# Pack attention fused with SwiGLU on one core: attention's products ahead of W's, half-products summed in place

## The chip, the cores and the metric

One core of a Trainium2 chip runs the whole program. The metric is device time in microseconds (us): the median of three executions. Beside it stands one profiled execution, in which every instruction of every engine has a start and a duration.

The engines are called PE (matrix products; PEld is its weight load), DVE (vector work), ACT (pointwise functions, casts, copies), POOL (slow vector work) and SP (which issues most transfers). Each runs its own instructions in a fixed order and waits at the first one whose inputs, or whose place for the result, are not ready.

## What is computed

```python
def sm_attn(qq, kk, vv):                       # 8 batches, 8 heads, head size 64
    s = scale * np.matmul(qq, kk.transpose(0, 1, 3, 2))
    s = s - np.max(s, axis=-1, keepdims=True)
    a = np.exp(s)
    a = a / (np.sum(a, axis=-1, keepdims=True) + 1e-09)
    return np.matmul(a, vv)
p_packed = sm_attn(p, k, v)                    # 32 pack rows look at 576 tokens
attn = sm_attn(q, p_packed, p_packed)          # 576 tokens look at 32 pack rows
x = attn of all heads side by side             # 4608 tokens x 512
g = x @ w_gate                                 # 512 x 1536
silu = g * (1.0 / (1.0 + np.exp(-g)))
out = (silu * (x @ w_val)) @ w_out             # 1536 x 512
```

All is float32. The large products are made from two parts of each operand, a rounded one ("high") and what is left of it ("low"), so three products stand for one.

## The kernel before

**Tiling.** The batches go through one after the other. Since the second attention has only 32 pack rows per head, its output is never formed: the packed rows are multiplied with w_gate and w_val first ("W's products", `m_mm`, 8 pairs of matmuls 32x512 at L293, result tile `aux`), split into `mh` (ACT, L669) and `ml` (DVE, L611), and the weights of attention `a2h`, `a2l` then multiply these (L712 in batch 1, L1092 from batch 2 on, result tile `gv`).

**Slots.** The inner dimension 1536 is cut into 12 pieces; piece fc of batch b is a slot. PE's order in a slot is written out by hand:

1. chunk a: 12 matmuls of 256 tokens into two banks (gate, val);
2. in odd slots (and in slot 11, for the next batch) W's products for the next pair of pieces;
3. in some slots products of the next batch's attention: q0 and q1 (scores of the pack rows, L433), pack (L517), mm0 and mm1 (scores of the tokens, L293 into `gv_aux`);
4. the first half of the output products of an earlier pair of pieces (`products(.., 0)`, 12 matmuls 256 wide, L1229, or in batch 1 `out_mm`, L731);
5. chunk b: 12 matmuls of 320 tokens into two banks;
6. the second half of the output products (`products(.., 1)`, 9 matmuls).

Behind a chunk ACT makes silu of the gate bank (`sg`, L719 or L1098) and DVE multiplies it with the val bank (`hf`, L723, or a quarter of the tiles `more` and `extra`, L1105).

**Banks.** Chunks, attention and W's products take their banks in turn from a ring of four, two at a time. In an odd slot that carries attention, chunk a has one pair, the next products the other pair, the products after these chunk a's pair again (so they wait for its silu and its product), and chunk b the other pair again (so it waits for the readers of whoever had it).

**Output products.** From batch 2 on, two pieces and two blocks of tokens form a 2x2 block product made from seven products instead of eight. Its left sides are four sums of quarters of the raw product (`ho`, from `split_raw`) and three (`hs`, from `split_sums`). POOL makes the sums, ACT the high part, DVE the low part. Before, POOL writes three of the sums to a tile `s_raw` of its own (L1188, L1197, L1198) and one in place (L1189). `ho` and `hs` have one buffer each.

**Who sets the order.** PE's order is the order of the code. The order on DVE, ACT and POOL is made by a scheduler from its own estimates, except for instructions under `pin`, which keep the order of the code among themselves. What attention does between the products is a table of words: `FIRST` for batch 2, `LATER` for the batches after it. A word's place "1.ha" means slot 1, after the whole of chunk a and its silu; "1.2" means the middle of slot 1, ahead of W's products. The words `q1r` and `q0r` are the readers of scores (maximum L448, subtraction L449, each twice), `block0` and `block1` those of mm0 and mm1 (L550).

**The tail.** Behind the last slot of batch 7 come seven pairs j = 0 to 6 whose two halves of output products are still to do, with five steps of a block of 64 left-over tokens of each batch pair between (`p4_step`, 6 matmuls 512 wide, L731), then `results` (DVE, L1259), and `end_out` (L733 to L749), which brings out the last 128 rows through two tiles x and y.

Of the kernel before, what the change touches and what calls it, by code (L numbers as in the profile page):

```python
# [25 lines left out]
P = 128  # L26
# [10 lines left out]
SCALE = 1.0 / 8.0  # L37
NW = 8 * P
SPLIT = 0
PAD = 0  # L40
QC = DM // 2

FRONT = 320
# [24 lines left out]
    0.2 q0  # L68
    0.4 q0r
    0.b q0s  # L70
    1.ha q1 q0e q1r
    1.6 q0z
    2.a q1e
    2.4 q1z
# [2 lines left out]
    4.2 factors  # L77
    4.5 turn0
    4.hb turn1
    5.ha pack  # L80
    5.b load_k
    6.a load_v
    6.8 tiles
    7.ha mm0 block0
    7.hb max0
    7.8 exp0
    8.1 sums0
    9.ha mm1 block1
# [10 lines left out]
"""  # L99

LATER = """
    -1.ha q0 q0r q0s
    -1.b q0e
    1.ha q1 q1r
    2.a q1e
    2.6 q0z
    2.b q1z
# [26 lines left out]
def tile_pack_attention_swiglu(ctx: ExitStack, tc: tile.TileContext, qT, q0, kT, v, vq, pT, wgv, wout, out):  # L134
# [22 lines left out]
    nc.scalar.activation(warm, zero, AF.Exp)  # L157

    w_t = [
        const.tile([P, NHP * 4 * P], F32, tag=f"w{k}", name=f"w{k}")[:, : NHP * 4 * P].rearrange(  # L160
            "p (h f n) -> p h f n", h=NHP, f=2
        )
        for k in range(NFC // 2)
# [646 lines left out]
    with tc.manual_schedule(engines={mybir.EngineType.PE}):  # L810
# [349 lines left out]
        late, s_raw, u_t, t4_parts = (None,) * 4  # L1160
        parts, accs = {}, {}

        def as_parts(x):
            return x.rearrange("p i (x n) -> p i x n", x=2)

        def open_late():
            nonlocal late, s_raw, t4_parts
            early_stack.close()
            late = ctx.enter_context(tc.tile_pool(name="late", bufs=1, reuse_waits="tile"))
            s_raw = late.tile([P, 3, P], F32, name="s_raw")  # L1170
# [6 lines left out]
        def part_tile(t, n):  # L1177
            x = late.tile([P, 2, n, P], F32R, tag=t, bufs=1, name=t)
            return x[:, 0], x[:, 1]

        def low(dst, src, high):
            nc.vector.tensor_tensor(dst, src, high.bitcast(F32), op=ALU.subtract)  # L1182

        def split_raw(at):

            x = raw[at]
            (a21, a11), (a22, _) = ([x[:, f, t] for t in range(2)] for f in range(2))
            nc.gpsimd.tensor_tensor(s_raw[:, 0], a21, a11, op=ALU.subtract)  # L1188
            nc.gpsimd.tensor_tensor(a21, a21, a22, op=ALU.add)  # L1189
            x = x.rearrange("p f t n -> p (f t) n")  # L1190
            hi, lo = parts[at, 0] = part_tile("ho", 4)
            nc.scalar.copy(hi, x)  # L1192
            low(lo, x, hi)

        def sum_raw(at):
            x = raw.pop(at)
            nc.gpsimd.tensor_tensor(s_raw[:, 1], x[:, 0, 0], x[:, 0, 1], op=ALU.subtract)  # L1197
            nc.gpsimd.tensor_tensor(s_raw[:, 2], x[:, 1, 1], s_raw[:, 1], op=ALU.subtract)  # L1198
            places.append(x)

# [9 lines left out]
        def t_quarter(k, i):  # L1210
            return ts[k][:, 0, i], ts[k][:, 1, i]

        def products(at, which, fill):
# [71 lines left out]
        def batch2(b):  # L1285
            nonlocal u_t, t4_parts
            run = plan_of(b)
            for fc in range(NFC):
# [32 lines left out]
                def half(which):  # L1321
# [36 lines left out]

# [40 lines left out]
```

## Time and profile before

| | us |
|---|---|
| median of three executions | 727.21 (725.76, 727.21, 727.58) |
| the profiled execution | 726.56 |
| its span, first to last instruction | 724.8 |
| outside the span (726.56 - 724.8) | 1.76 |
| PE busy in the span | 704.6 (97%) |
| DVE, ACT, POOL busy | 494.1, 403.1, 175.6 |
| mean granted clock of PE | 0.995 of full speed |

Time is read from the start of the span. PE is busy nearly always, so a change shows where PE stands still, where it runs at a lower clock, and at the very end. Where PE waits, the row of its next matmul says in brackets how long it stood and which instruction it waited for ("3.25 <-DVE e L449").

### The profile page before, as it was taken

How to read it: one execution, taken by the hardware profiler on the slowest of the kernel's cores; microseconds unless marked ns; L12 is line 12 of the kernel's file. 1: busy time of each engine (PE TensorE's matmuls, PEld its weight loads, DVE VectorE, ACT ScalarE, POOL GpSimd, SP SyncE). 2: the span in 40 equal slices, each digit the busy share in tenths (PEclk: the TensorE clock that was granted, in tenths of full speed). 3: DMA queues.
4: the chain of work that ended last, by engine and by line, in shares of the span. 5: the costliest groups of instructions: out<-in, count | busy, mean ns of one | idle time of the engine just before them, and what ended most of it. 6: DMA issues, size and time to landing. Idle time of an engine off the chain costs nothing.

```text
span 724.8 us, 16371 instructions
## 1 busy us (share of the span) xinstructions
PE 704.6 (97%) x6503; PEld 619.5 (85%) x6503; DVE 494.1 (68%) x1093; ACT 403.1 (56%) x714; POOL 175.6 (24%) x349
## 2 busy tenths in 40 slices
PE   7999999999979999999999999999999999999995
PEld 5687788888868999989989899898979989989985
DVE  4986876567856687677657776777746777555453
ACT  3788555635646475745736467655645456444331
POOL 0000000331452222322313323332312322233342
PEclk9999999999999999999999999999999999999999
DMA  9999993010250533434233441442405224210001
GB/s 347 359 350 318 335 419 125 7 73 13 105 186 8 200 124 119 158 143 162 99 126 107 168 171 64 165 182 88 182 17 173 93 88 175 89 60 30 1 30 44
DMA packets 25436, 103.27 MB, mean 142 GB/s; under 512 B 6672, under 2 KB 7952, under 8 KB 16656
## 3 DMA queue, kind: packets, MB, share of 16 engines
q1 hardware_dynamic: 25072, 102.00, 38.5%
q8 instruction: 51, 0.84, 0.5%
q10 hardware_dynamic: 288, 0.23, 0.1%
q14 instruction: 25, 0.20, 0.1%
HBM read 86.44 MB, written 15.78 MB: 141 GB/s over the span
## 4 chain that ended last, share of the span: by engine, by line
PE 89%; DVE 5%; ACT 2%; issue 2%; POOL 2%; DMA 0%; ACTq 0%; SPq 0%; DVEq 0%
PE gv L1092 31%; PE acc L1229 24%; PE acc L731 9%; PE aux L293 6%; PE gv L956 5%; PE gv L712 4%; PE aux L731 3%; PE gv_aux L293 1%; PE gv_aux L517 1%; PE warm_ps L817 1%; PE gv_aux L433 1%; DVE hs L1182 1%; DVE ot L1259 1%; ACT ho L1192 1%; PE gv_aux L854 0%
## 5 line engine op out<-in xcount | busy, mean ns | idle before, releaser
L1092 PE MATMUL gv<-a2h,ml 128*128 128x256 f32 (+1 forms) x576 | 124.5, 298 | 3.2 <-DVE e L449 3.2
L1092 PE MATMUL gv<-a2l,mh 128*128 128x256 f32 (+1 forms) x576 | 124.2, 297 | 0.0
L1092 PE MATMUL gv<-a2h,mh 128*128 128x256 f32 (+1 forms) x576 | 123.9, 296 | 0.0
L1092 PEld LDWEIGHTS gv<-a2h,ml 128*128 128x128 f32 x576 | 91.5, 189 | 4.7 <-issue 3.6
L1092 PEld LDWEIGHTS gv<-a2h,mh 128*128 128x128 f32 x576 | 93.4, 190 | 0.0
L1092 PEld LDWEIGHTS gv<-a2l,mh 128*128 128x128 f32 x576 | 93.2, 189 | 0.0
L611 DVE TENSOR_TENSOR ml<-aux,mh 128x512 fp32r<-128x512 f32 (+1 forms) x94 | 60.5, 676 | 32.6 <-ACT mh L669 32.5
L1203 ACT CAST hs<-s_raw 128x384 fp32r<-128x384 f32 x72 | 36.9, 512 | 76.4 <-PE acc L1229 70.4
L1098 ACT ACTIVATE sg<-gv 128x256 f32<-128x256 f32 (+1 forms) x144 | 59.2, 411 | 35.7 <-PE gv L1092 32.6
L669 ACT CAST mh<-aux 128x512 fp32r<-128x512 f32 (+1 forms) x94 | 50.0, 584 | 38.9 <-PE aux L293 38.4
L1229 PE MATMUL acc<-wo_h,ho 128*128 128x256 f32 x288 | 66.6, 294 | 2.2 <-DVE ho L1182 2.1
L1229 PEld LDWEIGHTS acc<-wo_h,ho 128*128 128x128 f32 x288 | 49.2, 188 | 18.3 <-issue 14.8
L1229 PE MATMUL acc<-t_w,hs 128*128 128x256 f32 x432 | 63.4, 282 | 0.0
L1229 PE MATMUL acc<-t_w,ho 128*128 128x256 f32 x432 | 62.8, 281 | 0.0
L1229 PEld LDWEIGHTS acc<-t_w,hs 128*128 128x128 f32 x432 | 58.6, 188 | 0.9 <-DVE ot L1259 0.2
L1188 POOL TENSOR_TENSOR s_raw<-more 128x128 f32<-128x128 f32 x36 | 16.7, 463 | 166.1 <-DVE hs L1182 163.9
L1229 PEld LDWEIGHTS acc<-t_w,ho 128*128 128x128 f32 x432 | 56.4, 188 | 0.2
L1182 DVE TENSOR_TENSOR hs<-s_raw,hs 128x384 fp32r<-128x384 f32 x72 | 39.6, 550 | 21.9 <-ACT hs L1203 20.8
L1188 POOL TENSOR_TENSOR s_raw<-extra 128x128 f32<-128x128 f32 x36 | 16.9, 469 | 142.3 <-DVE hs L1182 142.3
L1105 DVE TENSOR_TENSOR more<-gv,sg 128x256 f32<-128x256 f32 x72 | 30.1, 418 | 22.0 <-PE gv L1092 10.8
L1192 ACT CAST ho<-more 128x512 fp32r<-128x512 f32 x36 | 22.2, 618 | 33.0 <-PE acc L1229 26.1
L1229 PE MATMUL acc<-wo_l,ho 128*128 128x256 f32 x144 | 40.5, 282 | 0.0
(224 smaller groups left out, 1565.9 us busy)
## 6 DMA issues: line engine op xcount, KB each, us to landing
w_s<-wd SPq DMA_DIRECT2D x36, 1024.0 KB, 5.2
st<-in_wgv SPq DMA_DIRECT2D x12, 1024.0 KB, 7.6
k_t<-in_kT SPq DMA_DIRECT2D x16, 576.0 KB, 5.6
out<-ot SPq DMA_DIRECT2D x35, 256.0 KB, 2.2
q_t<-in_qT SPq DMA_DIRECT2D x14, 576.0 KB, 7.0
v_t<-in_vq SPq DMA_DIRECT2D x6, 1280.0 KB, 7.8
st<-in_wout SPq DMA_DIRECT2D x6, 1024.0 KB, 6.8
wd<-w SPq DMA_DIRECT2D x6, 1024.0 KB, 11.8
```

Source lines behind the costliest of these rows:

```text
L293: nc.tensor.matmul(outs[par][32 * hp : 32 * hp + 32], lhs(r, hp), rhs(r, hp), start=True, stop=True)
L611: pin(nc.vector.tensor_tensor(*x[1], op=ALU.subtract))
L669: nc.scalar.copy(m[0][at], src)
L731: nc.tensor.matmul(acc[:, at], h_[:, c : c + P], w_[fc // 2][:, fc % 2, at], start=((fc == 0 or first) and i == 0), stop=(fc == NFC - 1 an ...
L956: nc.tensor.matmul(held[i][s][:, :n], m_[:, g, f, s * P : (s + 1) * P], a_[:, g, off : off + n], start=(j == 0), stop=(j == len(todo) - 1),)
L1092: nc.tensor.matmul(pg[:, :n], m_[:, g, fc % 2, s * P : (s + 1) * P], a_[:, g, off : off + n], start=(i == 0), stop=(i == 5),)
L1098: nc.scalar.activation(sg[:, :n], pgs[0][:, :n], AF.Silu)
L1105: nc.vector.tensor_tensor(x, pgs[1][:, o : o + 256], sg[:, o : o + 256], op=ALU.mult)
L1182: nc.vector.tensor_tensor(dst, src, high.bitcast(F32), op=ALU.subtract)
L1188: nc.gpsimd.tensor_tensor(s_raw[:, 0], a21, a11, op=ALU.subtract)
L1203: nc.scalar.copy(hi, s_raw)
L1229: nc.tensor.matmul(acc[bank][:, QC * col : QC * col + QC], h_[:, x], w_, start=(k == 0 and i == 0 and col == 0), stop=(k == 5 and i == 2 a ...
```

## The change

Seven things are altered at once.

1. **Tables.** The places of q0, q1, pack, mm0 and mm1 go from "X.ha" to "X.2", in both tables. These products then stand ahead of W's products in the slot, and their readers ahead of `ml`.
2. **Sums in place.** `s_raw` is gone. POOL makes one sum in place (L1192), ACT and DVE make `ho` from the quarters, then POOL makes three sums in place (L1201), one after the other and only after DVE's low part has read the quarters; `hs` is made from these. The place in `more` or `extra` is given back only there. The columns of two products change accordingly.
3. **`split_sums`** is called ahead of chunk a rather than behind it.
4. **`pin_first`** keeps the code's order for the sums of the very first pair.
5. **Two buffers in the tail.** Pairs 1, 3 and 5 of the last half take their `ho` and `hs` from the buffers of `a2h` and `a2l`.
6. **The tail's left-over steps** move by one pair: none at j = 0, one at j = 5. `end_out` takes x and y from tiles no transfer reads any more.
7. **Addresses.** `PAD` is 40 instead of 0, and the tile of one weight block is 80 elements longer. Both only move tiles in memory.

```diff
 FIRST
-    1.ha q1 q0e q1r
+    1.2 q1 q0e q1r
-    5.ha pack
+    5.2 pack
...
 LATER
-    -1.ha q0 q0r q0s
+    -1.2 q0 q0r q0s
-    7.ha mm0 block0
+    7.2 mm0 block0
...
-        x, y = (pool.tile([P, DM], F32, tag="ot", bufs=2, name="ot") for _ in range(2))
+        x, y = (pool.tile([P, DM], F32, tag=t, bufs=1, name="ot") for t in ("a1", "s2"))
...
+        def part_tile(at, t, n):
+            if at[:2] == (B - 1, 1) and at[2] % 2:
+                x = pool.tile([P, 2, n, P], F32R, tag={"ho": "a2h", "hs": "a2l"}[t], bufs=2, name=t)
+            else:
+                x = late.tile([P, 2, n, P], F32R, tag=t, bufs=1, name=t)
...
+        def pin_first(at, ins):
+            return pin(ins) if at == (2, 0, 0) else ins
...
         def split_raw(at):
-            nc.gpsimd.tensor_tensor(s_raw[:, 0], a21, a11, op=ALU.subtract)
-            nc.gpsimd.tensor_tensor(a21, a21, a22, op=ALU.add)
+            x = raw[at].rearrange("p f t n -> p (f t) n")
+            pin_first(at, nc.gpsimd.tensor_tensor(x[:, 0], x[:, 0], x[:, 2], op=ALU.add))
...
         def sum_raw(at):
-            nc.gpsimd.tensor_tensor(s_raw[:, 1], x[:, 0, 0], x[:, 0, 1], op=ALU.subtract)
-            nc.gpsimd.tensor_tensor(s_raw[:, 2], x[:, 1, 1], s_raw[:, 1], op=ALU.subtract)
-            places.append(x)
+            for to, a, b in ((1, 0, 1), (3, 3, 1), (2, 1, 2)):
+                pin_first(at, nc.gpsimd.tensor_tensor(x[:, to], x[:, a], x[:, b], op=ALU.subtract))
...
+                if cur:
+                    split_sums(cur)
                 chunk(b, fc, False, fill, lambda: run(fc, "a"))
                 run(fc, "ha")
-                if cur:
-                    split_sums(cur)
...
-            if j < 5:
-                p4_step(j, B - 1)
+            if 0 < j < 6:
+                p4_step(j - 1, B - 1)
```

**ACT, batch 1, slot 1** (`sg` is silu of chunk a's gate bank, `e_1424` the exponentials of batch 2's first scores q0; a table load goes with each change of function). On PE, q1's row moves above W's in this slot.

```order
 L199 COPY ot<-acc 128x512
-L719 ACTIVATE sg<-gv 128x256
-L199 CAST hh<-hf 128x256
 L455 ACT_TABLE_LOAD
 L455 ACTIVATE e_1424<-e_1424 128x2x2x144
-L669 CAST mh<-aux 128x512 x2
 L719 ACT_TABLE_LOAD
+L719 ACTIVATE sg<-gv 128x256
+L199 CAST hh<-hf 128x256
+L669 CAST mh<-aux 128x512 x2
```

The exponentials and the load of silu's table now stand ahead of chunk a's silu.

**DVE, batch 2, slot 1, before**: the readers of q1's scores (L448, L449).

```order
L630 TENSOR_TENSOR b_t<-wo_h,wo_l 128x1024
L1105 TENSOR_TENSOR more<-gv,sg 128x256
L1182 TENSOR_TENSOR t_first<-t_593,t_first 128x256
L460 TENSOR_REDUCE z_2396<-e_2395 128x2x2
L448 TENSOR_REDUCE z_2396<-gv_aux 128x2
L1182 TENSOR_TENSOR hs<-s_raw,hs 128x384
L449 TENSOR_TENSOR e_2395<-gv_aux,z_2396 128x2x144
L448 TENSOR_REDUCE z_2396<-gv_aux 128x2
L1182 TENSOR_TENSOR t_first<-t_795,t_first 128x256
L449 TENSOR_TENSOR e_2395<-gv_aux,z_2396 128x2x144
L611 TENSOR_TENSOR ml<-aux,mh 128x512 x2
```

**DVE, the same place, of the change.**

```order
L630 TENSOR_TENSOR b_t<-wo_h,wo_l 128x1024
L1105 TENSOR_TENSOR more<-gv,sg 128x256
L1184 TENSOR_TENSOR t_first<-t_593,t_first 128x256
L460 TENSOR_REDUCE z_2373<-e_2372 128x2x2
L448 TENSOR_REDUCE z_2373<-gv_aux 128x2
L449 TENSOR_TENSOR e_2372<-gv_aux,z_2373 128x2x144
L448 TENSOR_REDUCE z_2373<-gv_aux 128x2
L449 TENSOR_TENSOR e_2372<-gv_aux,z_2373 128x2x144
L611 TENSOR_TENSOR ml<-aux,mh 128x512 x2
L1184 TENSOR_TENSOR t_first<-t_795,t_first 128x256
```

`hs` of the first pair no longer stands between the readers, and a left-over split has gone behind `ml`.

**ACT, the start of the tail, of the change** (silu of the last chunk b is the first row; `ho` and `hs` of three pairs follow).

```order
L1098 ACTIVATE sg<-gv 128x320
L1194 CAST ho<-extra 128x512
L1207 CAST hs<-more 128x384
L1249 COPY extra<-acc 128x256
L1207 CAST hs<-extra 128x384
L1250 COPY ot<-acc 128x256
L1194 CAST ho<-more 128x512
L1207 CAST hs<-more 128x384
```

The `ho` that PE needs next (from `more`) stands behind the `hs` of a pair that is needed later (from `extra`); before, it came straight after the two copies.

## Rows read from the trace of the kernel before

**Rows 1.** The page: DVE's group of ml (busy, mean ns, idle before it).
```profile
L611 DVE TENSOR_TENSOR ml<-aux,mh 128x512 fp32r<-128x512 f32 (+1 forms) x94 | 60.5, 676 | 32.6 <-ACT mh L669 32.5
```
**Rows 2.** Timeline of PE, batch 2, slot 1: start, duration, operation, count, [idle before].
```profile
209.42 0.40 PE L731 MATMUL acc<-wo_h,t_first 128*128 128x512 f32 x1
213.06 0.87 PE L1092 MATMUL gv<-a2h,ml 128*128 128x320 f32 x2 [3.25 <-DVE e L449]
...
216.30 0.40 PE L1092 MATMUL gv<-a2h,ml 128*128 128x256 f32 x2
```
**Rows 3.** The chain, 400 to 425 us: chunk b and two halves of output products.
```profile
409.14 1.77 PE gv L1092 x12
...
418.80 1.07 PE acc L1229 x9
...
421.31 1.42 PE acc L1229 x12
```
**Rows 4.** Timeline of DVE at the wait of rows 2.
```profile
208.79 0.44 DVE L448 TENSOR_REDUCE z<-gv_aux 128x2 f32<-128x288 f32 x1
211.99 0.56 DVE L1182 TENSOR_TENSOR hs<-s_raw,hs 128x384 fp32r<-128x384 f32 x1 [2.76 <-ACT hs L1203]
212.46 0.45 DVE L449 TENSOR_TENSOR e<-gv_aux,z 128x288 f32<-128x288 f32 x1
```
**Rows 5.** Timeline of PE, batch 1, slot 1.
```profile
120.82 1.09 PE L293 MATMUL aux<-w,ppt 64*32 64x512 f32 x16
121.70 0.75 PE L433 MATMUL gv_aux<-k_t,p_t 64*32 64x144 f32 x32
122.38 0.51 PE L731 MATMUL acc<-wo_h,hl 128*128 128x512 f32 x1
```
**Rows 6.** Timeline of ACT, the same slot.
```profile
120.26 0.38 ACT L719 ACTIVATE sg<-gv 128x256 f32<-128x256 f32 x1
...
121.88 1.28 ACT L455 ACT_TABLE_LOAD   x1
123.17 0.69 ACT L455 ACTIVATE e<-e 128x576 f32<-128x576 f32 x1
```
**Rows 7.** Timeline of PE, batch 1, slot 5.
```profile
147.75 1.96 PE L293 MATMUL aux<-w,ppt 64*32 64x512 f32 x16
...
150.29 1.31 PE L517 MATMUL gv_aux<-v_t,a 128*32 128x64 f32 x76 [0.34 <-DVE a L505]
151.53 0.50 PE L731 MATMUL acc<-wo_h,hl 128*128 128x512 f32 x1
```
**Rows 8.** Timeline of DVE, the same slot: the second transpose.
```profile
149.40 0.83 DVE L505 STREAM_TRANSPOSE a<-e 128x640 f32<-128x640 f32 x1
```
**Rows 9.** Windows: us; PE, PEld, DVE, ACT, POOL busy; granted clock; DMA share, GB/s.
```profile
213.00:216.50 3.50, 3.44 (x14) 3.47 (x15) 2.17 (x5) 0.64 (x2) 3.00 (x4) 0.55 0.45 174
...
713.00:717.00 4.00, 3.02 (x24) 3.02 (x25) 2.45 (x5) 1.24 (x3) 0.38 (x1) 1.00 0.00 0
```
**Rows 10.** Timeline of PE in the tail.
```profile
690.20 0.40 PE L731 MATMUL aux<-wo_h,t_parts 128*128 128x512 f32 x1
...
697.85 0.39 PE L1229 MATMUL acc<-wo_h,ho 128*128 128x256 f32 x1 [0.70 <-DVE ho L1182]
...
713.98 0.39 PE L1229 MATMUL acc<-wo_h,ho 128*128 128x256 f32 x1 [1.36 <-DVE ho L1182]
```
**Rows 11.** Timeline of ACT in the tail.
```profile
691.24 0.62 ACT L1192 CAST ho<-more 128x512 fp32r<-128x512 f32 x1 [0.82 <-POOL more L1189]
```
**Rows 12.** Timeline of DVE in the tail: low part of ho.
```profile
686.84 0.69 DVE L1182 TENSOR_TENSOR ho<-more,ho 128x512 fp32r<-128x512 f32 x1 [1.63 <-ACT ho L1192]
```
**Rows 13.** Timeline of POOL in the tail.
```profile
691.83 0.46 POOL L1198 TENSOR_TENSOR s_raw<-more,s_raw 128x128 f32<-128x128 f32 x1
```
**Rows 14.** Timeline of DVE at the end.
```profile
718.00 0.75 DVE L1259 TENSOR_TENSOR ot<-acc,ot 128x256 f32<-128x256 f32 x2
720.59 0.36 DVE L745 COPY ot<-aux 128x192 f32<-128x192 f32 x1 [1.83 <-DMA out<-ot]
```
**Rows 15.** Timeline of SP's queue at the end.
```profile
721.43 0.33 SPq L749 DMA_DIRECT2D out<-ot  x1
```

More of the change, by code (lines that the diff above doesn't have):

```diff
@@ L39 @@
 SPLIT = 0
-PAD = 0
+PAD = 40
 QC = DM // 2
@@ L87 @@
     8.1 sums0
-    9.ha mm1 block1
+    9.2 mm1 block1
     9.3 turn_0
@@ L101 @@
 LATER = """
-    -1.ha q0 q0r q0s
+    -1.2 q0 q0r q0s
     -1.b q0e
-    1.ha q1 q1r
+    1.2 q1 q1r
     2.a q1e
@@ L112 @@
     4.ha turn1
-    5.ha pack
+    5.2 pack
     6.7 tiles
-    7.ha mm0 block0
+    7.2 mm0 block0
     7.5 max0
@@ L120 @@
     8.hb turn_0
-    9.ha mm1 block1
+    9.2 mm1 block1
     9.5 high0
@@ L159, in tile_pack_attention_swiglu @@
     w_t = [
-        const.tile([P, NHP * 4 * P], F32, tag=f"w{k}", name=f"w{k}")[:, : NHP * 4 * P].rearrange(
+        const.tile([P, NHP * 4 * P + (80 if k == NFC // 2 - 1 else 0)], F32, tag=f"w{k}", name=f"w{k}")[:, : NHP * 4 * P].rearrange(
             "p (h f n) -> p h f n", h=NHP, f=2
@@ L1159, in tile_pack_attention_swiglu @@
         behind = batch1(1, behind)
-        late, s_raw, u_t, t4_parts = (None,) * 4
+        late, u_t, t4_parts = (None,) * 3
         parts, accs = {}, {}
@@ L1166, in open_late @@
         def open_late():
-            nonlocal late, s_raw, t4_parts
+            nonlocal late, t4_parts
             early_stack.close()
             late = ctx.enter_context(tc.tile_pool(name="late", bufs=1, reuse_waits="tile"))
-            s_raw = late.tile([P, 3, P], F32, name="s_raw")
             t4_parts = as_parts(late.tile([P, 2, 4 * P], F32R, tag="ho", bufs=1, name="t4_first"))
@@ L1175, in pair_at @@
             return (b + 2, r // 6, r % 6) if 0 <= b < B - 2 else None
-        def part_tile(t, n):
-            x = late.tile([P, 2, n, P], F32R, tag=t, bufs=1, name=t)
+        def part_tile(at, t, n):
[3 more added lines that the diff above has]
+                x = late.tile([P, 2, n, P], F32R, tag=t, bufs=1, name=t)
             return x[:, 0], x[:, 1]
         def low(dst, src, high):
-            nc.vector.tensor_tensor(dst, src, high.bitcast(F32), op=ALU.subtract)
+            return nc.vector.tensor_tensor(dst, src, high.bitcast(F32), op=ALU.subtract)
@@ L1184, in split_raw @@
+        def pin_first(at, ins):
+            return pin(ins) if at == (2, 0, 0) else ins
         def split_raw(at):
-            x = raw[at]
-            (a21, a11), (a22, _) = ([x[:, f, t] for t in range(2)] for f in range(2))
-            nc.gpsimd.tensor_tensor(s_raw[:, 0], a21, a11, op=ALU.subtract)
-            nc.gpsimd.tensor_tensor(a21, a21, a22, op=ALU.add)
-            x = x.rearrange("p f t n -> p (f t) n")
-            hi, lo = parts[at, 0] = part_tile("ho", 4)
-            nc.scalar.copy(hi, x)
@@ L1193, in split_raw @@
-            low(lo, x, hi)
+            x = raw[at].rearrange("p f t n -> p (f t) n")
+            pin_first(at, nc.gpsimd.tensor_tensor(x[:, 0], x[:, 0], x[:, 2], op=ALU.add))
+            hi, lo = parts[at, 0] = part_tile(at, "ho", 4)
+            pin_first(at, nc.scalar.copy(hi, x))
+            pin_first(at, low(lo, x, hi))
         def sum_raw(at):
-            x = raw.pop(at)
-            nc.gpsimd.tensor_tensor(s_raw[:, 1], x[:, 0, 0], x[:, 0, 1], op=ALU.subtract)
-            nc.gpsimd.tensor_tensor(s_raw[:, 2], x[:, 1, 1], s_raw[:, 1], op=ALU.subtract)
@@ L1199, in sum_raw @@
-            places.append(x)
+            x = raw[at].rearrange("p f t n -> p (f t) n")
+            for to, a, b in ((1, 0, 1), (3, 3, 1), (2, 1, 2)):
+                pin_first(at, nc.gpsimd.tensor_tensor(x[:, to], x[:, a], x[:, b], op=ALU.subtract))
         def split_sums(at):
-            hi, lo = parts[at, 1] = part_tile("hs", 3)
-            nc.scalar.copy(hi, s_raw)
-            low(lo, s_raw, hi)
+            place = raw.pop(at)
+            x = place.rearrange("p f t n -> p (f t) n")[:, 1:]
@@ L1206, in w_quarter @@
+            hi, lo = parts[at, 1] = part_tile(at, "hs", 3)
+            pin_first(at, nc.scalar.copy(hi, x))
+            pin_first(at, low(lo, x, hi))
+            places.append(place)
         def w_quarter(k, i, j):
@@ L1225, in products @@
             else:
-                todo = ((3, 0, 1, t_quarter(k, 3)), (3, 1, 0, t_quarter(k, 1)), (2, 1, 2, w_quarter(k, 1, 1)))
+                todo = ((3, 0, 0, t_quarter(k, 3)), (3, 1, 1, t_quarter(k, 1)), (2, 1, 2, w_quarter(k, 1, 1)))
             for n, (bank, col, x, (wh, wl)) in enumerate(todo):
```

## The prediction

> **What bounds the kernel now.** I read the page's shares first: PE is busy in 97% of the span (the table above). So another engine's work counts only where PE stands still for it, or where it stands behind PE's last product. The waits and the timeline of PE show where that is. The largest wait is in batch 2, slot 1: chunk b stands 3.25 us for a reader of scores [rows 2]. The timeline of DVE tells who is behind it: the reader L449 at 212.46 stands behind `hs` at 211.99, which had DVE idle for 2.76 [rows 4]. Then come the waits for `ho` in the tail, 0.70 and 1.36 [rows 10], and at the very end 1.83 of DVE behind a transfer [rows 14]. Last I read the slots in which the change reorders PE, for what the new order will wait for [rows 5 to 8].
>
> Durations are of the profiled execution, 726.56, of which 724.8 is span; that is 0.65 below the median of 727.21, well within 0.3% (2.2 us, about what a measurement of this kernel can tell from no change). The sum is made against 726.56.
>
> **A. Batch 2, slot 1: a gain of 4.3 (bounds 3.3 and 4.8).** In the new order of DVE no `hs` stands between the readers. The first L448 starts at 208.79 and takes 0.44, the L449 behind it 0.45 [rows 4], so the first scores are read by 209.7. PE's last product ahead of chunk b starts at 209.42 and hands over some 0.23 later (the pitch of these 512-wide products at full clock). Chunk b then starts at about 209.75 instead of 213.06: 3.3. Its matmuls also get cheaper. After the idle they take from 213.06 to 216.30 [rows 2], 3.24, where chunk b elsewhere takes 1.77 [rows 3]: the granted clock from 213 to 216.5 is 0.55 [rows 9], so most of it ran at 1.2 GHz. With no idle of 3 us ahead of it I take 1.77, another 1.47. Something comes back: the readers end at 210.6, two `ml` of 0.676 [rows 1] at about 211.95, and chunk a of the next slot needs them, while chunk b now ends at 211.5: minus 0.45. Sum 3.3 + 1.47 - 0.45 = 4.3. The lower bound leaves the clock out (3.3), the upper one the wait for `ml` (4.8).
>
> **B. Batch 1, slot 1: a loss of 2.0 (bounds 0.9 and 2.4).** Today W's products start at 120.82, q1 at 121.70, the output products at 122.38 [rows 5]. Now q1 is first and ends at 121.5. W's first result lies in q1's first bank and waits for its reader, 0.44 + 0.45 later [rows 4]: 122.4. W's second result lies in chunk a's bank and waits for silu. On ACT the exponentials now stand ahead of that silu: ACT comes free at about 120.2, where silu starts today, then a table load 1.28, the exponentials 0.6 up to the next start, a load back 1.28, silu 0.38 [rows 6]: 123.8. The part of W's that is left takes some 0.55, about two thirds of 0.88 (121.70 - 120.82), so the output products start at 124.4 instead of 122.38. The lower bound is a silu that is there in time: 122.4 + 0.88 = 123.3, a loss of 0.9. The upper one adds 0.4 for DVE, which may bring the reader later.
>
> **C. Batch 1, slot 5: a loss of 0.9 (bounds 0.8 and 2.4).** pack waits for the second transpose, which ends at 149.40 + 0.83 = 150.23 [rows 8]. Today W's fill the time ahead of that: pack stands only 0.34 and runs from 150.29 to 151.53 [rows 7], 1.24. Now pack is first; it would start at 147.75 [rows 7], where W's start today, and wait to 150.23, but for a first part of a few short matmuls. So PE stands some 2.3 us, and W's 0.88 come behind: 150.29 + 1.24 + 0.88 = 152.4 against 151.53. The upper bound adds 1.5 for a clock that falls in that idle.
>
> The trace shows idle of 1.36 [rows 10], behind which the clock stayed at 1.00 (2.4 GHz; 713 to 717) [rows 9], and idle of 3.25 [rows 2], behind which it was 0.55 [rows 9]. The new waits of B, C and E lie between, and no row decides. The Trainium skill, "TensorE: Matmul & The Clock Gate", section "Part 1: The HAM clock gate (the "warmup" mystery)", says that the throttled state is the default and that activity releases it. By that rule a wait long enough would cost once more behind its end, at most 4.5 over the three places, and the sum would be near nothing. I take the upper level for the forecast; the lower one is a rival below.
>
> **D. The other slots with q0, q1, pack, mm0, mm1: a gain of 0.5 (bounds a loss of 1.5 and a gain of 1).** In batches 2 to 6 some 24 such slots change order. W's products now wait for chunk a's product where attention did (0.1 to 0.2 a slot either way), and attention's readers get the time of W's and of the output products before chunk b wants their bank; W's bank is read later by `mh` and `ml`. No such slot shows a wait of PE above 0.4 today beside the one of A, so a gain is bounded by small waits, a loss by 1.5 (0.06 a slot). I take 0.5, near the gain of the small waits. The order of `hs`, later behind POOL's three subtractions, is hidden by 12 + 9 matmuls of output products, 1.42 + 1.07 [rows 3].
>
> **E. The tail: a gain of 1.0 (bounds 0 and 2.2).** Waits for `ho` of 0.70 and 1.36 [rows 10] go, since `ho` and `hs` have two buffers and the split no longer waits for PE to read the last one; with small ones like them and the slow restarts behind them 3.2 in all. A new one comes at j = 1. Up to now a left-over step starts at 690.20 [rows 10] and covers the split; now there is none at j = 0, so the second half of its products ends at 690.20 + 1.07 [rows 3] = 691.3, and so PE comes to j = 1 then. Its `ho` needs, on ACT, an `hs` of another pair first; that waits for POOL's three subtractions of that pair, which I put to about 691.4 from POOL's pitch of 0.54 (691.83 - 0.46 [rows 13] is the end of the one before, 0.07 apart). Then 0.5 for `hs`, 0.62 for `ho` [rows 11], 0.69 for the low part [rows 12]: about 693.5, a wait of 2.2. It takes the place of 3.2: gain 1.0. If POOL is done 1 us sooner the gain is 2.2; if other copies on ACT come between, it is 0.
>
> **F. The end: a gain of 1.5 (bounds 1.2 and 1.7).** DVE's last copy waits 1.83 for a transfer that still reads the tile [rows 14], and the last transfer goes out at 721.43 [rows 15]. With x and y in other tiles the copies start when the results do: these end at 718.00 + 0.75 [rows 14], then a copy and a sum of 0.36, then the issue: about 719.7. That is 1.7 earlier, less up to 0.5 for the transfers that now lie closer together.
>
> The addresses (`PAD`, the longer tile) I cost at nothing: no row depends on an address. `split_sums` ahead of chunk a is costed in A and D, `pin_first` in A.
>
> Sum: 4.3 - 2.0 - 0.9 + 0.5 + 1.0 + 1.5 = 4.4. 726.56 - 4.4 = 722.2; the median lies 0.65 above the profiled time: **722.8**.
>
> **Rivals.**
> *The new waits are smaller.* If silu comes in time in B (a loss of 0.9) and POOL is ahead in E (a gain of 2.2): 722.8 - 1.1 - 1.2 = 720.5. For it: both terms rest on an order of ACT whose start times shift. Against it: the exponentials need a table load each way [rows 6].
> *The clock falls behind the new waits.* B, C and E each leave PE idle for about 2 us or more. By A's rows each fall costs 3.24 - 1.77 = 1.5. One fall gives 724.3, two 725.8, three 727.3. For it: 3.25 did it; against it: 1.36 did not.
> *The stall of A stays in another form.* The change may not do what it says: if the second reader is late for another cause, for instance the first scores' tiles come by a late transfer, pack or chunk a waits the same 3 to 4 us a little later. Then 722.8 + 4 = 726.8. For it: the next wait is always behind the first one. Against it: the chain in [rows 4] names only `hs`.
> *W's too late in its slot: slower.* W's stand behind attention, so `mh` and `ml` come later, and the next slot's chunk a waits for them. From the end of W's, PE has 1.42 + 1.77 + 1.07 = 4.25 of other products [rows 3]. DVE needs two readers ahead (4 x 0.45 = 1.8) and 2 x 0.676 = 1.35 for `ml` behind ACT's `mh`, in all some 3.2: spare about 1. If DVE is more than 1 us behind in these slots, each of the 16 slots with q0, q1, mm0 or mm1 in batches 2 to 6 loses some 0.45 (the size of one reader): 7.2, 722.8 + 7 = 730. For it: ml's group is the one that always waits for `mh` [rows 1]. Against it: DVE is busy two thirds of the time.
>
> **How the numbers follow.** My forecast, 722.8 with an own range of 721.0 to 724.6: 0.60. Smaller waits, 720.5: 0.17. The clock falls: 0.10, about half of it below 725. The stall in another form: 0.08. Slower: 0.05. Faster by over 0.3% is below 725.03: 0.60 + 0.17 + 0.05 = 0.82. Slower is above 729.39: 0.05. The same: 0.13. The range leaves out 0.05 above with the slower case and a few hundredths of the stall, and about a quarter of the better case: 720.3 to 726.0.
>
> **What would show it.** Right: in batch 2, slot 1, no wait of PE over 1 us and chunk b at 1.77. In batch 1, slot 1, W's products in two pieces, waiting for L449 and for silu, output products some 2 us later against chunk a. In slot 5 of batch 1 a wait of about 2.3 ahead of pack. In the tail one wait at j = 1 for `ho` and none later; at the end no DVE wait for a transfer. Wrong: chunk a waiting for `ml` or `mh` in many slots of batches 2 to 6; a granted clock below 1.00 behind the new waits; a wait for pack or a late score in batch 2.

## The result: slower by 1.1%

The changed kernel takes 734.79 (median; 733.37 to 736.43) against 727.08 in the same comparison, a ratio of 1.0108 with a 95% interval of 1.0091 to 1.0124. The forecast was 722.8 with a range of 720.3 to 726.0. The profiled execution has a span of 734.0 against 724.8, 9.2 more. By the medians it is 7.7: the profiled execution of the changed kernel (735.78) lies 1.0 above its median, the one of the kernel before (726.56) 0.5 below. The table and the rows below are of these two executions; the paragraphs on B and C say what differs from execution to execution.

To find where, I took the start of each of the 187 chunks (unbroken rows of matmuls into `gv`) in both traces, in order, and subtracted. The difference from one chunk to the next is what was lost or won between them:

| part of the prediction | foretold | measured |
|---|---|---|
| before batch 1, slot 1 | nothing | 0.7 gained |
| A: batch 2, slots 1 to 3 | 4.3 gained | 4.2 gained |
| B: batch 1, slot 1 | 2.0 lost | 4.1 lost |
| C: batch 1, slot 5 | 0.9 lost | 2.65 lost |
| rest of batch 1 | nothing | 0.1 lost |
| D: batches 2 to 7 behind A | 0.5 gained | 9.4 lost |
| E: the tail, up to PE's last matmul | 1.0 gained | 0.3 gained |
| F: from there to the end of the span | 1.5 gained | 1.8 gained |

D alone turns the sum around. The waits of PE in the changed kernel (who for whom, us in total, times, longest; the first line, at the very start of the span, and the smaller ones left out) don't look like it:

```profile
...
PE gv_aux L517 <- DVE a L505: 2.4, 1, 2.4
PE aux L293 <- DVE more L1105: 1.8, 3, 0.7
PE acc L1234 <- DVE ho L1184: 1.5, 1, 1.5
PE aux L293 <- DVE e L449: 1.2, 1, 1.2
PE aux L293 <- DVE extra L1105: 1.1, 4, 0.3
PE acc L1234 <- DVE hs L1184: 0.5, 1, 0.5
...
```

The 3.2 for L449 of the kernel before [rows 2] is gone. In its place W's products (L293) wait in eight slots, in all but one of them for under 0.8. No wait for `ml` or `mh` is among them, so the slower rival of the prediction (chunk a waiting for these) did not happen; its 730 is the nearest of the forecasts, but by another cause. The table of waits shows only a part: PE's busy time rose from 704.6 to 715.4, and in the slot shown below two of W's matmuls, while one waits for its bank, count as 1.04 of busy time, about as much as all 16 undisturbed (1.09).

**A, nearly as foretold.** PE, batch 2, slot 1. Chunk b follows the output products without a wait and takes 217.69 - 215.94 = 1.75, where it took 3.24 [rows 2]:

```profile
215.94 0.45 PE L1092 MATMUL gv<-a2h,ml 128*128 128x320 f32 x2
...
217.69 0.42 PE L1092 MATMUL gv<-a2h,ml 128*128 128x256 f32 x2
```

**D, the slot that loses most.** Batch 4, slot 11, with q0, one of four such slots that lose 1.27 each. First PE and DVE of the kernel before, where W's products are first:

```profile
439.99 1.09 PE L293 MATMUL aux<-w_s,ppt 64*32 64x512 f32 x16
440.87 0.75 PE L433 MATMUL gv_aux<-k_t,p_t 64*32 64x144 f32 x32
441.55 0.39 PE L1229 MATMUL acc<-wo_h,ho 128*128 128x256 f32 x1
```
```profile
439.07 0.77 DVE L591 STREAM_TRANSPOSE t<-s 128x576 f32<-128x576 f32 x1
439.76 0.52 DVE L1182 TENSOR_TENSOR hs<-s_raw,hs 128x384 fp32r<-128x384 f32 x1
440.20 0.41 DVE L1105 TENSOR_TENSOR extra<-gv,sg 128x256 f32<-128x256 f32 x1
```

`extra`, DVE's product that frees chunk a's val bank, ends 0.62 after W's start (440.61 - 439.99). W's 0.88 cover that, and q0 follows without a wait: 1.56 from 439.99 to the output products. The same slot of the changed kernel, PE, DVE, ACT and POOL:

```profile
447.30 0.72 PE L433 MATMUL gv_aux<-k_t,p_t 64*32 64x144 f32 x32
447.86 1.04 PE L293 MATMUL aux<-w_s,ppt 64*32 64x512 f32 x2
449.17 1.09 PE L293 MATMUL aux<-w_s,ppt 64*32 64x512 f32 x14 [0.27 <-DVE extra L1105]
450.19 0.39 PE L1234 MATMUL acc<-wo_h,ho 128*128 128x256 f32 x1
```
```profile
447.56 0.56 DVE L1184 TENSOR_TENSOR hs<-more,hs 128x384 fp32r<-128x384 f32 x1 [0.85 <-ACT hs L1207]
448.04 0.77 DVE L591 STREAM_TRANSPOSE t<-s 128x576 f32<-128x576 f32 x1
448.73 0.38 DVE L1105 TENSOR_TENSOR extra<-gv,sg 128x256 f32<-128x256 f32 x1
```
```profile
447.01 0.52 ACT L1207 CAST hs<-more 128x384 fp32r<-128x384 f32 x1 [1.07 <-POOL more L1201]
```
```profile
445.15 1.83 POOL L1201 TENSOR_TENSOR more<-more 128x128 f32<-128x128 f32 x3 [3.34 <-DVE r L577]
```

Read it from the bottom: POOL's three sums end at 446.98, ACT's `hs` starts at 447.01, DVE's `hs` at 447.56 after 0.85 of standing still, and behind it wait the transpose and `extra`. In the kernel before the transpose came first and `hs` waited for nothing. `extra` now ends 1.81 (449.11 - 447.30) after the first matmul behind chunk a instead of 0.62, and W's last 14 matmuls, which need its bank, come out 1.08 later, at 450.19: 2.89 instead of 1.56.

### The profile page after: what moved, and what is told of

It reads as the page before. It is cut to its first block, busy times and chain, and to the rows that moved or that the text cites. A ratio compares the mean times of both kernels' runs of the same rounds, so it can differ in the third digit from the quotient of the medians.

```text
span 734.0 us, 16288 instructions
## 1 busy us (share of the span) xinstructions
PE 715.4 (97%) x6503; PEld 613.1 (84%) x6503; DVE 497.1 (68%) x1093; ACT 398.9 (54%) x714; POOL 184.4 (25%) x349
## 4 chain that ended last, share of the span: by engine, by line
PE 84%; DVE 6%; ACT 4%; POOL 3%; issue 2%; DMA 1%; DVEq 0%; ACTq 0%
PE gv L1092 26%; PE acc L1234 23%; PE acc L731 9%; PE aux L293 8%; PE gv L956 5%; PE gv L712 4%; PE aux L731 3%; POOL more L1201 2%; PE gv_aux L293 1%; PE gv_aux L517 1%; DVE ho L1184 1%; PE warm_ps L817 1%; DVE ot L1264 1%; DMA st<-in_wout 1%; ACT L569 1%
## 5 line engine op out<-in xcount | busy, mean ns | idle before, releaser
L1092 PE MATMUL gv<-a2h,ml 128*128 128x256 f32 (+1 forms) x576 | 122.5, 294 | 0.0
L1092 PE MATMUL gv<-a2l,mh 128*128 128x256 f32 (+1 forms) x576 | 122.1, 293 | 0.0
L1092 PE MATMUL gv<-a2h,mh 128*128 128x256 f32 (+1 forms) x576 | 121.6, 292 | 0.0
L1092 PEld LDWEIGHTS gv<-a2h,mh 128*128 128x128 f32 x576 | 91.6, 188 | 0.0
L1201 POOL TENSOR_TENSOR extra<-extra 128x128 f32<-128x128 f32 x108 | 55.7, 529 | 127.5 <-DVE ho L1184 109.2
L1201 POOL TENSOR_TENSOR more<-more 128x128 f32<-128x128 f32 x108 | 54.1, 514 | 126.5 <-DVE ho L1184 103.1
L293 PE MATMUL aux<-w_s,ppt 64*32 64x512 f32 x576 | 57.3, 600 | 3.0 <-DVE more L1105 1.8
L1207 ACT CAST hs<-extra 128x384 fp32r<-128x384 f32 x36 | 18.5, 513 | 51.1 <-POOL extra L1201 42.0
L1207 ACT CAST hs<-more 128x384 fp32r<-128x384 f32 x36 | 18.5, 513 | 49.6 <-POOL more L1201 49.4
L731 PE MATMUL acc<-wo_h,hl 128*128 128x512 f32 x96 | 39.9, 416 | 0.0
```

The lines of the kernel that those rows point to most:

```text
L293: nc.tensor.matmul(outs[par][32 * hp : 32 * hp + 32], lhs(r, hp), rhs(r, hp), start=True, stop=True)
L731: nc.tensor.matmul(acc[:, at], h_[:, c : c + P], w_[fc // 2][:, fc % 2, at], start=((fc == 0 or first) and i == 0), stop=(fc == NFC - 1 an ...
L1092: nc.tensor.matmul(pg[:, :n], m_[:, g, fc % 2, s * P : (s + 1) * P], a_[:, g, off : off + n], start=(i == 0), stop=(i == 5),)
L1201: pin_first(at, nc.gpsimd.tensor_tensor(x[:, to], x[:, a], x[:, b], op=ALU.subtract))
L1207: pin_first(at, nc.scalar.copy(hi, x))
```

## The experiments

Three theories stood against each other. **M**: `hs` on DVE stands ahead of `extra` and waits for POOL, and whoever is second on PE pays. **T**: the order of the tables alone is the loss; **S**: the sums in place alone.

**e1: the tables back.**
```diff
-    1.2 q1 q0e q1r
+    1.ha q1 q0e q1r
...
-    -1.2 q0 q0r q0s
+    -1.ha q0 q0r q0s
```
(and pack, mm0, mm1 in both tables, q1 in the second)

> The changed kernel with all ten places of the tables back at X.ha, so that W's products stand ahead of attention's again; sums in place, tail, end and addresses stay as changed. The changed kernel shows three kinds of loss: 4.07 in slot 1 and 2.65 in slot 5 of batch 1, and about 9.5 in the slots of batches 2 to 6 with q0 (1.27 each), mm1 (0.71), mm0 (0.36) and q1 (0.14 to 0.31). Theory M (both parts together: W's second product waits for the product of chunk a's val bank, which DVE now makes later because hs stands ahead of it and waits for POOL; the order of the tables only exposes it): the 6.7 of batch 1 goes, and of the 9.5 about 5.5, since W's 0.88 cover more of the wait than q0's 0.56; some 0.9 for each of four q0 slots stays: 734.8 - 12.2 = 722.6. Theory T (the tables alone cause it): all 16.2 goes, 718.6. Theory S (the sums in place alone cause the loss in the slots): 734.8 - 6.7 = 728.1. The stall of batch 2, slot 1 stays away in all three, since hs does not come back between the readers of the scores.

Measured: 728.62, ratio to before 1.0015 (1.0001 to 1.0029). By the total S looks right; by slots it does not. B and C are gone, and q0 loses 0.90 as M has it. But slot 1 of batches 4 and 6 loses 3.8 and 2.6 to something new. PE and DVE there (batch 4):

```profile
372.40 1.21 PE L433 MATMUL gv_aux<-k_t,p_t 64*32 64x144 f32 x30 [1.75 <-DVE ot L201]
```
```profile
371.65 0.69 DVE L201 COPY ot<-aux 128x512 f32<-128x512 f32 x1 [1.49 <-DMA out<-ot]
```

A copy that empties the bank of left-over rows waits for its tile's transfer, and behind PE's 1.75 the granted clock is 0.50 (from 372 to 375). Without those 6.4 the run stands at 722.2, against 722.6 foretold by M; the subtraction is mine, and e8 is the run without them.

**e2: the tables alone, on the kernel before** (the diff of e1 the other way round).

> The kernel before with the ten new places of the tables and nothing else of the change. Theory M: batch 1 loses its 6.7; the product of chunk a's val bank stays as early as before (0.6 after chunk a's end), so the q0 slots lose some 0.2 instead of 1.27, mm0 and mm1 lose as in the changed kernel (5.5 in all): 727.1 + 6.7 + 6.3 = 740, the stall of 3.25 in batch 2 staying. Theory T: 727.1 + 6.7 + 9.5 = 743.3. Theory S: 727.1 + 6.7 = 733.8.

Measured: 734.72, ratio 1.0103 (1.0076 to 1.0130), though batch 1 loses its 2.5 and 2.6. q0 loses 0.14, as M says; mm1 loses 0.17, where M had it lose 0.7 as in the changed kernel. The total is lower than M's 740 mostly for that (2.7 in five slots) and since B costs 2.5 instead of 4.1 here. The stall of A shrank by itself a little: `hs` stands there ahead of the second reader's L449 alone, so chunk b starts 3.05 earlier, but its second bank waits 2.01 for that reader, and 2.28 goes again up to the next slot's chunk b.

**e3: the first table back** (batch 1's places only).

> The changed kernel with the places of the first table (batch 2's attention, run in batch 1) back at X.ha; the second table as changed. All theories: slots 1 and 5 of batch 1 give back 4.07 and 2.65 if the order of q1, pack and W's there is the cause, and mm0 and mm1 of the batch after about 1: 734.8 - 7.7 = 727. If something else of the change slows batch 1 (addresses, transfers): above 730.

Measured: 730.06, ratio 1.0036 (1.0018 to 1.0054). In the trace slots 1 and 5 of batch 1 are as before (0.04 gained, 0.09 lost), so B and C come from the first table. The slots of batches 2 to 6 lose as in the changed kernel; the 1.0 that I had added for mm0 and mm1 was wrong, since those of batches 2 to 6 hang on the second table. By the two profiled executions the run is 6.8 below the changed kernel, by the medians 4.7: B's 4.1 is not in every execution, as the paragraph on B shows.

**e4: the split of the three sums back behind chunk a.**
```diff
-                if cur:
-                    split_sums(cur)
                 chunk(b, fc, False, fill, lambda: run(fc, "a"))
                 run(fc, "ha")
+                if cur:
+                    split_sums(cur)
```

> The changed kernel with the split of the three sums back behind chunk a in the code's order, which puts hs behind the transpose or behind the product of chunk a's val bank on DVE in the slots with q0, mm0 and mm1. Theory M: the product comes up to 0.6 earlier in the q0 slots and in some of the mm1 slots, so 1.27 falls to about 0.6 in four slots: 734.8 - 2.7 = 732; hs later may cost as much where the output products wait for it. Theory T: no gain, 734.8. Theory S (POOL's three subtractions are the bound): no gain either, 734.8.

Measured: 732.17, ratio 1.0067 (1.0046 to 1.0088): 2.6 less than the changed kernel by the medians, 4 times 0.66 by the q0 slots, M's 2.7. DVE and PE in the slot of above:

```profile
444.84 0.77 DVE L591 STREAM_TRANSPOSE t<-s 128x576 f32<-128x576 f32 x1
445.78 0.56 DVE L1184 TENSOR_TENSOR hs<-more,hs 128x384 fp32r<-128x384 f32 x1 [0.17 <-ACT hs L1207]
446.26 0.42 DVE L1105 TENSOR_TENSOR extra<-gv,sg 128x256 f32<-128x256 f32 x1
```
```profile
446.09 1.73 PE L293 MATMUL aux<-w_s,ppt 64*32 64x512 f32 x16
447.75 0.39 PE L1234 MATMUL acc<-wo_h,ho 128*128 128x256 f32 x1
```

The transpose now fills the time in which `hs` waited for POOL (0.17 instead of 0.85), and the slot loses 0.61. mm1 does not gain: there the scheduler had the transpose ahead of `hs` already.

**e8: both back**, the tables and the place of `split_sums`.

> The changed kernel with the tables back and the split of the three sums back behind chunk a: of what bears on the slots only the sums in place are left. With the tables alone back, the q0 slots still lost 0.90 each against before, mm1 0.35, and two q1 slots stood for a copy that waits for its tile (6.4 in all). If the loss of q0 and mm1 comes from where hs stands on DVE (ahead of the product of chunk a's val bank): q0 falls to 0.3 or less, 728.6 - 2.4 = 726.2, less if the two waits for the copy go too, down to 720. If it comes from POOL's later subtractions whatever the place: q0 stays at 0.9, 728.6.

Measured: 720.04, ratio 0.9907 (0.9890 to 0.9923): faster than the kernel before. q0 loses 0.2, and the two waits for the copy are gone. What each kind of slot loses, from chunk to chunk:

| slot (how many) | tables (e2) | sums in place (e1) | both (changed) | both, hs behind (e4) | sums, hs behind (e8) |
|---|---|---|---|---|---|
| q0 (4) | 0.14 | 0.90 | 1.27 | 0.61 | 0.2 |
| mm1 (5) | 0.17 | 0.35 | 0.71 | 0.72 | 0.35 |
| mm0 (5) | 0.37 | 0 | 0.36 | 0.36 | 0 |
| q1 (4) | 0.15 to 0.3 | 0.4 or the copy | 0.15 to 0.3 | 0.15 to 0.3 | 0 |

These are the values of batches 3 to 6 (q0: 2 to 5); mm0 and mm1 of batch 2, so soon behind A, differ by up to 0.4.

**e13: the tables on a kernel without the stall** (e11, below, with the new places).

> The kernel of e11 with the ten new places of the tables: what the tables cost by themselves where neither the sums in place nor the stall of batch 2 is in the way. By the slots of the run with the tables only: 2.5 and 2.6 in slots 1 and 5 of batch 1, 0.8 in the rest of that batch, and in batches 2 to 6 q0 0.14, mm1 0.17, mm0 0.37, q1 0.17 to 0.31 each, 3.8 in all: 719.7 + 9.7 = 729.4. If in those slots the tables cost 1.27, 0.7, 0.36 and 0.2 as in the changed kernel (9.5): 735.

Measured: 727.93, ratio 1.0016 (1.0000 to 1.0033), 8.2 above e11 (9.7 foretold). In its profiled execution, 10.9 above that of e11, 6.6 lie in slots 1 and 5 of batch 1, B's 4.1 among them. In batches 2 to 6 q0 loses 0.12 to 0.15, mm0 0.37, mm1 0.17 to 0.19: the small numbers of e2 again.

**e10: only the stall of A taken away**, on the kernel before, by pinning `hs` of the first pair.
```diff
-            nc.scalar.copy(hi, s_raw)
-            low(lo, s_raw, hi)
+            pin_first(at, nc.scalar.copy(hi, s_raw))
+            pin_first(at, low(lo, s_raw, hi))
```

> The kernel before; only hs of the very first pair (its cast on ACT and its low part on DVE) keeps the order of the code, so that it no longer stands between the two readers of q1's scores in batch 2, slot 1. Theory: the stall there (3.25 of idle and 1.5 of chunk b at the lower clock) goes without the tables: 727.3 - 4.6 = 722.7. Rival: the next wait takes its place (hs late for its own products, or chunk a behind ml): 725 or more.

Measured: 723.37, ratio 0.9953 (0.9936 to 0.9970). The stall is gone and gives 4.1 of the 4.6; mm1 of batch 2 takes 0.6 back. So A needs neither the tables nor the sums in place.

**e5: only the end's tiles.**
```diff
-        x, y = (pool.tile([P, DM], F32, tag="ot", bufs=2, name="ot") for _ in range(2))
+        x, y = (pool.tile([P, DM], F32, tag=t, bufs=1, name="ot") for t in ("a1", "s2"))
```

> The kernel before with one line of the change: x and y of the end are taken from tiles that no transfer reads any more. In the changed kernel the stretch from PE's last product to the end of the span is 5.0 instead of 6.8. If the line alone is the cause: 1.8 less, 725.7. If the transfers of the end collide and give it back: 0.5 less or nothing.

Measured: 725.95, ratio 0.9986 (0.9977 to 0.9996): 1.0 less. From the start of PE's last matmul to the end it is 5.6 here and 6.8 before; in the changed kernel 5.0. In both the last transfer goes out 1.5 after that start. The other 0.6 lies behind this issue: from it to the end of the span it takes 4.1 here and 3.5 in the changed kernel (3.3 before, 3.5 in e11, 4.1 in e13). What makes that difference is open.

**e11 and e12: the tail.** e11 is the kernel before with the pin, the end's tiles and two buffers for `ho` and `hs`; e12 also shifts the left-over steps.
```diff
-            if j < 5:
-                p4_step(j, B - 1)
+            if 0 < j < 6:
+                p4_step(j - 1, B - 1)
```

> The kernel before with the pin of the first pair's hs, the end's tiles, and two buffers for ho and hs in the tail, without the shift of the left-over steps, without the tables and without the sums in place. Theory (the parts add): 727.3 - 4.6 - 1.8 = 720.9, and the tail's waits for ho (2.9 by the excess of matmul starts) go in part: 718.5 to 720.9. Rival: the scheduler's new order in the tail brings a wait like that of 1.47 at pair 1 of the changed kernel: 721 to 722.5.

> The kernel of e11 (before with the pin, the end's tiles and two buffers in the tail) with the tail's left-over steps shifted by one pair as in the changed kernel. Theory: with no step at pair 0, ho of pair 1 comes late and PE stands some 1.5 to 2.2 there, while the 0.7 that e11 still shows for ho goes: 719.7 + 0.8 to 1.5 = 720.5 to 721.2. Rival: the shift is what two buffers are for, and the last wait goes without a new one: 719.0.

Measured: 719.69 (ratio 0.9897, 0.9880 to 0.9913) and 721.02 (0.9918, 0.9903 to 0.9933). From the last matmul of the last chunk to PE's last matmul: 30.4 before, 28.4 with two buffers, 30.2 with the shift too, 30.1 in the changed kernel. The buffers give 2.1 and the shift takes 1.9 of it (1.3 by the medians). PE's one wait for `ho` in the tail of e11, and that of the changed kernel at pair 1 with ACT there:

```profile
694.08 0.39 PE L1235 MATMUL acc<-wo_h,ho 128*128 128x256 f32 x1 [0.69 <-DVE ho L1185]
```
```profile
705.01 0.39 PE L1234 MATMUL acc<-wo_h,ho 128*128 128x256 f32 x1 [1.47 <-DVE ho L1184]
```
```profile
702.92 0.51 ACT L1207 CAST hs<-extra 128x384 fp32r<-128x384 f32 x1 [1.21 <-POOL extra L1201]
703.34 0.37 ACT L1250 COPY ot<-acc 128x256 f32<-128x256 f32 x1
703.60 0.62 ACT L1194 CAST ho<-more 128x512 fp32r<-128x512 f32 x1
```

As foretold, `ho` stands on ACT behind `hs` of another pair, which waits for POOL.

**e14 and e15: the best version, and the addresses.** e14 is e8 with the left-over steps where they were; e15 is e14 with `PAD` 0 and no longer tile.

> The kernel of e8 (the changed kernel without the tables and with the split of the three sums behind chunk a) with the left-over steps of the tail where they were before: at pairs 0 to 4. Two buffers without the shift left 28.4 from the last chunk to PE's last product, with the shift 30.2. If the shift is what costs it here too: 720.0 - 1.8 = 718.2. If POOL's three subtractions behind the low part hold up the tail by themselves: 720.0.

> The kernel of e14 with the addresses of the kernel before: PAD 0 and the weight block's tile not longer. In all runs with the change's addresses and sums in place each of some 40 chunks a is 0.06 shorter than in the kernel before, some 2 us over batches 2 to 7; in the runs without them it is not. If the addresses do it: 718.5 + 2 = 720.5, and a chunk a of 256 tokens takes 1.52 up to the next product instead of 1.47. If the sums in place do it, or nothing of the change: 718.5, chunks as before.

Measured: e14 718.54, ratio 0.9877 (0.9861 to 0.9894), faster than both kernels. e15 721.14, ratio 0.9912 (0.9895 to 0.9928). The addresses are worth 2.6. A chunk a in e14 and in e15, with the matmul behind it:

```profile
468.60 0.40 PE L1092 MATMUL gv<-a2h,ml 128*128 128x256 f32 x2
...
469.97 0.28 PE L1234 MATMUL acc<-wo_h,ho 128*128 128x256 f32 x1
```
```profile
470.05 0.40 PE L1092 MATMUL gv<-a2h,ml 128*128 128x256 f32 x2
...
471.49 0.28 PE L1234 MATMUL acc<-wo_h,ho 128*128 128x256 f32 x1
```

1.37 against 1.44; in each of the chunks a of batches 2 to 7 it is some 0.06. The addresses alone on the kernel before were not tried.

**e6: the two banks of W's products swapped.**
```diff
-        pss = m_ps[b, k, fcs.start] = [ps(), ps()]
+        pss = m_ps[b, k, fcs.start] = [ps(), ps()][::-1]
```

> The changed kernel with the two banks of W's products swapped, so that the first of the 16 matmuls and not the second writes the val bank of chunk a. The changed kernel shows the first matmul alone, then the second alone after about 0.45, then the other 14. If a wait inside the run of 16 costs a matmul's time of its own (0.45) because the eight row and column parts no longer go side by side: four q0 slots and five each of mm0 and mm1 lose up to 0.45 less, in all up to 5.8: about 729 to 731. If only the arrival of the val bank counts, and the split of the run lies inside that wait: 734.8, no change.

Measured: 735.53, ratio 1.0116 (1.0098 to 1.0134), and the same three pieces of W's products in the trace (1, 1 and 14 matmuls, the last behind the same 0.27 for `extra`). So the edit did not move the wait to the first matmul; why not is not shown. Whether the broken run of 16 costs anything was not settled by it. The rows of the changed kernel say that it costs little: from `extra`'s end at 449.11, 14 matmuls are done 1.08 later, against 0.88 for all 16 undisturbed.

## Why the prediction was wrong

**A held**, 4.2 for 4.3. The wait gives 3.26 (3.3 foretold) and the clock 1.49 (1.47), and e10 shows that the cause was the one named. The 0.45 that comes back is right by luck: the next chunk a does not wait for `ml`, as the sum had it. In its place 0.53 goes in slot 3, where W's products take 1.68 instead of 1.13: there DVE's last reader of the chunk b ahead (L1108) ends 0.52 after W's start, and before it ended ahead of it.

**D failed, and it is the cause of the wrong sign.** The step was one sentence: that `hs` comes later behind POOL's three subtractions "is hidden by 12 + 9 matmuls of output products". That answers who needs `hs` on PE. It does not ask what stands behind `hs` on DVE. There stand the transpose and `extra`, and PE's next products need the bank that `extra` frees. e4 and e8 show it: with `hs` behind the transpose q0 loses 0.61 instead of 1.27 and 0.2 instead of 0.90.

D also priced the tables' half wrongly, at 0.1 to 0.2 "either way". With r the time from the first matmul behind chunk a until the val bank is free, W first ends at max(0.88, r) + 0.68, and W second at max(0.56, r) + 1.02, by the rows above. For r = 0.62 that is 1.56 and 1.64, for r = 1.82 it is 2.50 and 2.84. So by these rows the longer product in second place never wins; it pays 0.1 where the bank is early and 0.34 where it is late: measured 0.14 (e2) and 0.37 (1.27 - 0.90).

The traces give the same for mm0 and mm1. PE and DVE of the changed kernel in batch 4, slot 9 (mm1):

```profile
434.16 1.73 PE L293 MATMUL aux<-w_s,ppt 64*32 64x512 f32 x16
435.82 0.39 PE L1234 MATMUL acc<-wo_h,ho 128*128 128x256 f32 x1
```
```profile
433.86 0.56 DVE L1184 TENSOR_TENSOR hs<-extra,hs 128x384 fp32r<-128x384 f32 x1 [0.17 <-ACT hs L1207]
434.33 0.42 DVE L1105 TENSOR_TENSOR more<-gv,sg 128x256 f32<-128x256 f32 x1
```

mm1's first matmul is at 433.54, so r is 1.21 and the output products come after 2.28; before, the same two are 0.61 and 1.50, and `hs` waits for nothing. So `hs` behind POOL is in mm1 too. In mm0's slot 7 r is 1.33 before and 1.38 in the changed kernel, and the products come after 2.03 and 2.45: the bank was late already, and the order alone costs there.

The four kinds of slot in the changed kernel add to 11.5. Of these the sums in place, with `split_sums` ahead of chunk a, make 5.4 by themselves (q0 and mm1 in e1), the tables alone 4.0 (e2), and some 2 come only when both meet: W's products second, and the bank late. The shorter chunks of the new addresses take 2.0 back, which leaves the 9.4. Two readings were wrong beside this: D has no wait of PE above 0.4 in such slots, but in the kernel before q1 of batches 4 and 6 waits 0.72 for `ml`; and the slower rival's 16 slots are 18 (the table at e8).

None of this was among the signs. A, B, C, E and F nearly all showed what the prediction called right; for D it named only chunk a waiting for `ml` or `mh`, and no sign for W's own products waiting. The sign of wrong that did come, the clock, cost some 3.2 in B and C together.

**B: the wait for silu was right, what comes behind it was not.** Silu is late by two table loads, as foretold (one of them in the rows), and W's products wait for it. PE and ACT:

```profile
122.05 2.97 PE L293 MATMUL aux<-w,ppt 64*32 64x512 f32 x16 [1.19 <-DVE e L449]
124.94 0.79 PE L731 MATMUL acc<-wo_h,hl 128*128 128x512 f32 x1
```
```profile
121.48 1.28 ACT L719 ACT_TABLE_LOAD   x1
122.77 0.38 ACT L719 ACTIVATE sg<-gv 128x256 f32<-128x256 f32 x1
```

Of five profiled executions with this order three lose 2.5 (e2, e4, e6; 2.0 foretold, upper bound 2.4) and two lose 4.1 (the changed kernel, e13). In the three the 0.5 more is the part of W's products that is left behind silu: 14 of 16 matmuls, 1.07 in e2 instead of the 0.55 of the sum. The windows tell why the two lose 1.6 more: granted clock (third number from the end) from 124 to 126 in the changed kernel and in e2.

```profile
124.00:126.00 2.00, 2.00 (x17) 0.86 (x4) 0.76 (x2) 1.00 (x3) 0.00 (x0) 0.50 0.69 264
```
```profile
124.00:126.00 2.00, 2.00 (x15) 1.42 (x9) 1.35 (x3) 1.21 (x3) 0.00 (x0) 1.00 0.75 289
```

**C was mis-sized by its clock.** PE, and the window behind the wait, in the changed kernel:

```profile
153.57 1.85 PE L517 MATMUL gv_aux<-v_t,a 128*32 128x64 f32 x76 [2.38 <-DVE a L505]
155.35 1.96 PE L293 MATMUL aux<-w,ppt 64*32 64x512 f32 x16
157.24 0.64 PE L731 MATMUL acc<-wo_h,hl 128*128 128x512 f32 x1
```
```profile
153.50:155.50 2.00, 1.93 (x84) 1.76 (x92) 1.50 (x4) 0.00 (x0) 1.84 (x3) 0.67 0.00 0
```

The wait is 2.38 (2.3 foretold), but behind it pack takes 1.78 up to the next instead of 1.24 and W's 1.89 instead of 0.88: together the 1.5 of the upper bound, and a little more. It was so in all five profiled executions, 2.55 to 2.65. The Trainium skill, "TensorE: Matmul & The Clock Gate", section "Part 1: The HAM clock gate (the "warmup" mystery)", says that the throttled state is the default. The trace agrees behind C in these five, and behind B in two of them. So the price of a fall, 1.5, was right, and 0.10 for it was too little. It does not fall in every execution: the four of the changed kernel have mean granted clocks of 0.995, 0.996, 0.993 and 1.000, and the last is the fastest (733.37).

**E had both mechanisms and the wrong net**: 0.3 instead of 1.0. The buffers give 2.1 (e11). I had put the old waits at 3.2, of which the two waits in the rows are 2.06 and the rest stood on no row. The shift costs 1.9 (e12). I had 2.2, but the terms as written (691.4 + 0.5 + 0.62 + 0.69) add to 693.2 and not to 693.5, which gives 1.9.

**F held**: 1.8 (1.5 foretold, a little over its bound of 1.7). DVE and SP's queue: no wait for a transfer, and the last issue 1.5 after the last matmul's start, where it was 3.4 [rows 15]:

```profile
728.89 0.35 DVE L745 COPY ot<-aux 128x192 f32<-128x192 f32 x1
```
```profile
730.50 0.58 SPq L749 DMA_DIRECT2D out<-ot  x1
```

**The addresses** were costed at nothing and are worth 2.6 (e14 against e15). No row of the kernel before could have told, but it was a place for a bound, not for a zero.

## What to carry to other kernels

When an operation is made later, list what stands behind it on its own in-order engine before asking who needs its result; here the two were different, and the second list was harmless. Where two groups of products share a ring of banks and the second waits for a bank, try the longer one first; here that order was never the slower one. Give every term of the sum its own sign of being wrong, the small ones too. And when two gains and a reordering come as one change, price them one by one: the parts of this one without the tables, without the shift and with `hs` in its old place are 1.2% faster than the kernel before, while the whole is 1.1% slower.

## What the runs showed of the hardware

- Two paddings, of 160 and 320 bytes in a partition, which move the tiles behind them, shorten each chunk a by some 0.06 (in the rows of e15 and e14 from 1.44 to 1.37); chunk b keeps its pace (within 0.02). Which operand does it, and why, is open.
- Behind PE idle of 2.4 the granted clock was lower in five of five profiled executions (0.67 in the window shown), and behind waits of 1.75 (e1) and 2.01 (e2) too (0.50 and 0.54), where 1.36 had left it alone [rows 9, 10]; behind a wait of 1.19, followed by a few matmuls waiting for silu, it was lower in two of five. One execution of the changed kernel has a mean of 1.000, so the 2.4 seem not to lower it always; that execution has no trace.
- POOL's three sums in place took 1.83 in the slot shown: two took 0.46 each, as a sum before [rows 13], and the one between them 0.88, while DVE ran an operation with two inputs (L582, 445.49 to 446.24). Over all 216 the mean is 0.52. The Trainium skill, "SBUF — State Buffer", section "SBUF: two separate sides", says that an operation of POOL and one of DVE with two inputs in that memory lock each other out; the one slow sum agrees with it, though no run here separates it.
